# Key and value projections of a gated attention/MLP mix as units of seven block products, spilled and reloaded

## The chip, the cores and the metric

The kernel runs on one core of one Trainium2 chip. The metric is device time in microseconds (us) of one execution, given as the median of several runs; less is better. A profile shows one profiled execution: its span is the time from its first to its last instruction, and names such as L237 are lines of the kernel before.

## What is computed

The reference, cut to what matters (2048 tokens x 1024 channels, 32 heads of 32 channels, 3584 MLP channels, all in float32):

```python
x = A_x
g = _sigmoid((x * gate_w).sum(-1, keepdims=True))
q, k, v = split_heads(x @ wqkv)
pq, pk = q @ w_phi, k @ w_phi                      # per head
phi_q = concat([softmax(pq), softmax(-pq)])        # per head, 64 features
phi_k = concat([softmax(pk), softmax(-pk)])
kv = einsum("bhsf,bhsd->bhfd", phi_k, v)           # sum over all tokens
z  = einsum("bhsf->bhf", phi_k)
a = (phi_q @ kv / (phi_q @ z + 1e-6)) @ wo
b = (gelu(x @ w_gate) * (x @ w_up)) @ w_down
return g * a + (1 - g) * b
```

The features of every query need kv and z, which are sums over all 2048 tokens.

## The kernel before, in words

**Numbers.** Each float32 operand is split into a high part (rounded, written by ScalarE: `high`, L573, or `split`, L47) and a low part (the rest, written by VectorE: `low`, L576, or L48). A matrix product runs in three passes (`PASSES`, L24): high x high, high x low, low x high. One matmul has a stationary 128x128 block and 512 moving columns.

**Three stages.** The first stage (L165 to L560) projects keys and values. For each half of the heads (`hh`, L367) the weights for keys are folded with the feature map w_phi by small float32 matmuls (`fold`, L220) and stay split in SBUF; then sixteen chunks of 128 tokens are projected with the tokens on the output partitions (`keys_values`, L234: 8 blocks of channels x 3 passes x 2 column parts of 512). As the outputs are born in PSUM with tokens on partitions, `features` (L243) takes max, min, exponentials and normalisation right there, sums the features into `zacc` for z, and `accumulate` (L269) multiplies them with the values into four PSUM banks. The second stage projects queries, gate and up. The third multiplies by wo and w_down (L1189 on) and adds the gated results.

**Units of seven products.** In stages two and three a product of 2 x 2 blocks is made with seven block products instead of eight, from sums of blocks of x, of weights and of results (`x_sums` L174, `quarter_sums` and `more_sums` L156 to L163). A unit (`unit`, L947) is one pair of 128-channel column tiles of one weight (gate "g", up "u", query "q") for one half of the tokens (1024): seven calls of `product` (L908), each with 12 matmuls, so 84. Its weight operands are called x, y, z (1024 columns, split) and v (512). There are 64 units: half 0, then half 1, each 14 gate, 14 up and 4 query units. Operands of x for a half are four plain quarters (`xb`) and four sums (`xs`); at the turn `second_half` (L747) loads and splits those of half 1.

**What sets the order.** In stages two and three the order on TensorE (PE), VectorE (DVE), ScalarE (ACT) and SyncE (SP, which issues loads) is written out by a planner at build time. Time is counted in slots of one product, seven slots a unit. `run_slot` (L671) puts work of generator streams into each slot by estimated costs: `weights` (L789) prepares the operands of a unit from seven slots ahead to four slots behind its start, with due slots; `results` (L916) takes the products out; `background` (L1002) does work without a due slot when it fits, above all `attention` (L1042), a job for each of 8 head groups x 2 token blocks x 2 halves, 32 in all. Small matmuls of attention are "fillers" put into slots. What is left after the last unit runs in `drain` (L863), with no products beside it. In the second pass (half 1) the weight sums of the first pass are read back unsplit from HBM (`right_sums`) and split again. Spills to HBM go through GpSimd (POOL). The attention jobs read their queries back with `load_query` (L1033).

## Time and profile before

| | |
|---|---|
| median of 3 runs | 2352.43 us (2352.29 to 2352.74) |
| span of the profiled execution | 2351.2 us, 28278 instructions |
| HBM traffic | read 337.51 MB, written 109.58 MB, 190 GB/s |
| DMA packets | 156426, of these 22208 under 512 bytes |

The results give no separate device time for the profiled execution; its span lies 1.2 us under the median. On the page, an engine's line gives busy time, share of the span and number of instructions; a line of digits gives the busy tenths in 40 equal slices; PEclk is the clock granted to TensorE. A group's line reads: line, engine, operation, output tile <- input tiles, shapes, count, then total busy us and mean ns of one, then the idle time of the engine ahead of them and what ended it. In a row of windows the columns are the stretch, its length, then busy us (and instructions) of PE, PE weight loads, DVE, ACT and POOL, the granted clock, the DMA engines' busy share and GB/s.

### The profile page before, as it was taken

What the parts mean: (1) busy time and instruction counts of PE and PEld (TensorE: products, weight loads), DVE (VectorE), ACT (ScalarE), POOL (GpSimd) and SP (SyncE); (2) the same over time, 40 slices, a digit from 0 to 9 for tenths busy, and PEclk for the clock granted to TensorE, in tenths of its full rate; (3) what the DMA queues carried; (4) which work ended last, traced back from release to release, by engine and by line L of the source; (5) the groups of instructions that cost most, each with busy time, mean ns of one, the idle gap of its engine ahead of it and who ended that gap; (6) DMA issues with size and microseconds to landing.
All of it is one profiled execution on the core that took longest, in us unless ns stands there. A gap on an engine that the chain in (4) does not pass through costs nothing.

```text
span 2351.2 us, 28278 instructions
## 1 busy us (share of the span) xinstructions
PE 2346.5 (100%) x10594; PEld 1952.7 (83%) x10594; DVE 1808.1 (77%) x2356; ACT 1049.8 (45%) x1377; POOL 179.6 (8%) x334
## 2 busy tenths in 40 slices
PE   9999999999999999999999999999999999999999
PEld 8888888888888888888888888888888888888887
DVE  7997898887887777678778787787664868867874
ACT  4323223655555554456565655655533222323221
POOL 0000020211111111110001000000000000000000
PEclk9999999999999999999999999999999999999999
DMA  7322652645444655574444444444874767977874
GB/s 280 125 81 81 208 203 105 229 145 189 157 176 149 210 193 204 184 258 140 140 149 153 135 144 148 135 144 140 285 263 153 277 225 254 347 260 273 285 268 136
DMA packets 156426, 448.71 MB, mean 191 GB/s; under 512 B 22208, under 2 KB 24512, under 8 KB 155264
## 3 DMA queue, kind: packets, MB, share of 16 engines
q1 hardware_dynamic: 125664, 346.40, 44.2%
q0 software_dynamic: 29952, 100.17, 10.7%
q8 instruction: 83, 1.36, 0.2%
q10 hardware_dynamic: 672, 0.33, 0.1%
q14 instruction: 55, 0.45, 0.1%
HBM read 337.51 MB, written 109.58 MB: 190 GB/s over the span
## 4 chain that ended last, share of the span: by engine, by line
PE 100%; DVE 0%; issue 0%
PE po L1359 29%; PE a L913 22%; PE pd L237 15%; PE c L913 15%; PE b L913 7%; PE p L913 7%; PE pg L273 1%; PE misc L1132 1%; PE pd L609 0%; PE pd L150 0%; PE pg L225 0%; PE pd L225 0%; PE pd L197 0%; DVE x L1312 0%; DVE ones L187 0%
## 5 line engine op out<-in xcount | busy, mean ns | idle before, releaser
L237 PE MATMUL pd<-wkv,x 128*128 128x512 f32 x1536 | 358.6, 391 | 0.0
L237 PEld LDWEIGHTS pd<-wkv,x 128*128 128x128 f32 x1536 | 286.0, 188 | 57.4
L1359 PE MATMUL po<-tw,wgu 128*128 128x512 f32 x1344 | 309.8, 389 | 0.0
L1359 PEld LDWEIGHTS po<-tw,wgu 128*128 128x128 f32 x1344 | 252.3, 188 | 52.4
L573 ACT ACTIVATE wgu<-stage 128x1024 fp32r<-128x1024 f32 x146 | 154.2, 1056 | 245.3 <-DVE stage L1249 161.9
L576 DVE TENSOR_TENSOR wgu<-stage,wgu 128x1024 fp32r<-128x1024 f32 x146 | 177.8, 1218 | 83.0 <-ACT wgu L573 82.0
L576 DVE TENSOR_TENSOR tyz<-stage,tyz 128x1024 fp32r<-128x1024 f32 x129 | 156.9, 1216 | 67.9 <-ACT tyz L573 67.6
L913 PE MATMUL a<-s,tyz 128*128 128x512 f32 x768 | 184.6, 389 | 0.0
L913 PE MATMUL a<-s,v 128*128 128x512 f32 x768 | 184.5, 389 | 0.0
L913 PE MATMUL c<-x,tyz 128*128 128x512 f32 x768 | 184.5, 389 | 0.0
L913 PE MATMUL a<-x,wgu 128*128 128x512 f32 x756 | 181.7, 389 | 0.0
L913 PE MATMUL p<-s,tyz 128*128 128x512 f32 x756 | 181.6, 389 | 0.0
L913 PE MATMUL c<-x,wgu 128*128 128x512 f32 x756 | 181.6, 389 | 0.0
L913 PE MATMUL b<-s,tyz 128*128 128x512 f32 x756 | 181.6, 389 | 0.0
L913 PEld LDWEIGHTS a<-s,tyz 128*128 128x128 f32 x768 | 144.1, 188 | 30.1 <-ACT c L958 0.2
L913 PEld LDWEIGHTS a<-s,v 128*128 128x128 f32 x768 | 144.2, 188 | 29.9
L913 PEld LDWEIGHTS c<-x,tyz 128*128 128x128 f32 x768 | 144.2, 188 | 29.9
L913 PEld LDWEIGHTS p<-s,tyz 128*128 128x128 f32 x756 | 141.9, 188 | 29.5
L913 PEld LDWEIGHTS b<-s,tyz 128*128 128x128 f32 x756 | 141.9, 188 | 29.4
L913 PEld LDWEIGHTS c<-x,wgu 128*128 128x128 f32 x756 | 141.9, 188 | 29.5
L913 PEld LDWEIGHTS a<-x,wgu 128*128 128x128 f32 x756 | 141.8, 188 | 29.4
L1359 PE MATMUL po<-tw,wl 128*128 128x512 f32 x672 | 156.9, 389 | 0.0
(195 smaller groups left out, 3455.4 us busy)
## 6 DMA issues: line engine op xcount, KB each, us to landing
stage<-lm SPq DMA_DIRECT2D x98, 512.0 KB, 4.5
sr<-in_w_down SPq DMA_DIRECT2D x84, 512.0 KB, 5.1
sl<-lm SPq DMA_DIRECT2D x70, 512.0 KB, 4.7
lm<-h POOLq DMA_DIRECT2D x112, 256.0 KB, 2.3
stage<-in_w_gate SPq DMA_DIRECT2D x43, 512.0 KB, 3.7
stage<-in_w_up SPq DMA_DIRECT2D x43, 512.0 KB, 3.6
tg<-stage POOLq DMA_DIRECT2D x28, 512.0 KB, 2.9
tu<-stage POOLq DMA_DIRECT2D x28, 512.0 KB, 3.4
```

The costliest lines, as they stand in the source:

```text
L237: nc.tensor.matmul(ps[m], xb[b, kc // 4][:, a, kc % 4, t * P:(t + 1) * P], w[:, e, m * 512:(m + 1) * 512], start=kc == 0 and (a, e) == (0, ...
L273: nc.tensor.matmul(pkv[d // 2][:, d % 2], vs[:, d].rearrange("p a b -> p (a b)"), f[:, :, :, heads], start=first and d % 2 == 0, stop=last ...
L573: nc.scalar.activation(dst, src, AF.Copy)
L576: nc.vector.tensor_tensor(dst, src, dst_h.bitcast(F32), OP.subtract)
L913: nc.tensor.matmul(dst, w[:, h, 4 * part + kc, :], xq[:, e, kc, :], start=first and kc == 0 and i == 0, stop=kc == 3 and i == 2, skip_grou ...
L1132: nc.tensor.matmul(po[p], kbs[:, p].rearrange("p i a b -> p (i a b)"), pts[:, q, p, :], start=q == 0, stop=q == 1)
L1359: nc.tensor.matmul(ps[c], lefts[s][:, a, m, c * P:(c + 1) * P], made[k][:, e, m], start=d == 0 and m == 0 and n == 0, stop=d == n_duo - 1 ...
```

## The change

Keys ("k") and values ("v") become units like gate, up and query: four pairs of column tiles x two halves each. Their results are spilled to HBM with channels on partitions and brought back with tokens on partitions, by DMAs in pieces of 32 numbers plus 32x32 block transposes on VectorE. The list of units is now: half 0 v and k, half 1 v and k, half 1 gate/up/query, half 0 gate/up/query, so the operands of x change halves twice (`change_half`, the old `second_half`, is called at both turns). Unit 0 is a plain product (8 blocks of channels, no sums) run while x arrives and is summed. Behind it stand the folds of the key weights (`fold_piece`), in part within unit 1, and the first splits. The query folds, the gate's dot products, the sums of half 1 and the features of keys (`features`, now 32 jobs) are streams under the units; z is summed by accumulating DMAs into HBM and reduced in `finish_z`; `attention` waits for all of that. In `attention` the first steps of a job move to a stream of their own (`front`), and the four exponentials are placed one by one. The first pass of each weight pair stores y, z and v split; a second pass reads them back ready, and splits only x. The diff is cut to its core; what was in the first stage is left out.

```diff
+        for s in range(KC):
+            kc, i = kcs[s], s // 2
+            w_high, w_low = weight_part(s, 1 if s < 2 else 2) if s < 2 or s % 2 == 0 else (lambda: None, lambda: None)
+            xq = {blk: x_plain(blk, kc) for blk in range(2)}
+            src = {blk: raws[i][2 - 2 * blk + s % 2] for blk in range(2)}
+            w_high()
+            high(xq[1][:, 0], src[1])
+            if s == 0:
+                nc.vector.tensor_copy(xq[0][:, 0], src[0])
+            else:
+                high(xq[0][:, 0], src[0])
+            for blk in (1, 0):
+                low(xq[blk][:, 1], src[blk], xq[blk][:, 0])
+            w_low()
+            if s >= 2:
+                sum_steps(1)
+            if s % 2:
+                ready.append(i)
+            if s == 3:
+                for h in range(2):
+                    t = fp.tile([P, 4, 4, 32], F32, tag=f"vs{h}", name="bp", bufs=1)
+                    nc.vector.tensor_tensor(t, phi_c[:, 4 * h:4 * h + 4].unsqueeze(2).to_broadcast([P, 4, 4, 32]),
+                                            mask.unsqueeze(1).to_broadcast([P, 4, 4, 32]), OP.mult)
+                    bps.append(t)
+            for n, (a, e) in enumerate(PASSES):
+                for blk in (1, 0):
+                    for f in range(2):
+                        nc.tensor.matmul(plain_banks[blk, f], wide_w[a][:, kc, f * P:(f + 1) * P], xq[blk][:, e],
+                                         start=s == 0 and n == 0, stop=s == KC - 1 and n == 2)
...
+        def fold_piece(i):
+            h, kc = order[i]
+            s, pf = homes[i], misc()
+            for j in range(4):
+                nc.tensor.matmul(pf[:, j * P:(j + 1) * P], s[:, j * P:(j + 1) * P],
+                                 bps[h][:, j].rearrange("p a b -> p (a b)"), start=True, stop=True)
+            high(s, pf)
+            nc.gpsimd.dma_start(wk_fold[h][kc], s)
+            if 5 <= i < 12:
+                fold_load(i + 4)
...
+        sum_steps(100)
+        fold_piece(0)
+        plain_out(0, 1, 0)
+        fold_piece(1)
+        plain_out(1, 0, 1)
+        high(flat(x1)[0], first_e)
+        low(flat(x1)[1], first_e, flat(x1)[0])
+        fold_piece(2)
+        plain_out(2, 0, 0)
+        quarter_sums(first_e, first_o)
+        high(flat(y1)[0], first_o)
+        fold_piece(3)
+        plain_out(3, 1, 1)
+        low(flat(y1)[1], first_o, flat(y1)[0])
+        nc.gpsimd.dma_start(sums["v", 1]["y"], y1.rearrange("p a b c -> p (a b c)").bitcast(F32))
...
+        def plain_out(n, j, f):
+            high(results_0[:, n], plain_banks[j, f])
+            nc.gpsimd.dma_start(spilled["v"][0][f][j], results_0[:, n])
...
+        def more(n, m):
+            for _ in range(n):
+                x_highs.pop(0)()
+            for _ in range(m):
+                x_lows.pop(0)()
...
+        more(2, 0)
+        fold_piece(4)
+        more(2, 4)
+        fold_piece(5)
+        more(3, 3)
+        more_sums(first_e, first_o)
+        z1 = slot()
+        high(flat(z1)[0], first_e)
+        fold_piece(6)
+        low(flat(z1)[1], first_e, flat(z1)[0])
+        nc.gpsimd.dma_start(sums["v", 1]["z"], z1.rearrange("p a b c -> p (a b c)").bitcast(F32))
+        more(9, 9)
 
...
+        for half in (0, 1):
+            units += [(half, k, m) for k in "vk" for m in range(N_Q)]
+        for half in (1, 0):
             mine = [(half, k, m) for m in range(NF // 2) for k in "gu"]
             for m in range(N_Q):
-                mine.insert((0, 7, 12, 19)[m] if half else 7 * m, (half, "q", m))
+                mine.insert((0, 7, 12, 19)[m], (half, "q", m))
             units += mine
-
-        right_ops = {}
+        TURNS = [n for n in range(1, len(units)) if units[n][0] != units[n - 1][0]]
...
+            def load_parts(i, t):
+                nc.sync.dma_start(t.rearrange("p a b c -> p (a b c)").bitcast(F32), sums[kind, m][i])
             if n == 1:
-                ke, e, ko, o = 0, second_raw[0], 1, second_raw[1]
+                mine.update(x=x1, y=y1, z=z1)
             else:
-                while not room(2):
+                yield t - 7, t - 6, 0.0
+                while not room(1 + fresh):
                     yield now[0] + 1, t - 5, 0.0
-                ke, e = hold((0, 1024, w[2 * m]))
-                ko, o = hold((0, 1024, w[2 * m + 1] if fresh else right_sums[kind, m][0]))
-            yield t - 5, t - 3, 0.0, 1.05
-            x = new_weight() if n > 1 else xa.tile([P, 2, KC, P], F32R, tag="pts", name="second", bufs=1)
-            xh, xl = flat(x)
-            high(xh, e)
-            yield now[0] + 1, t - 2, 1.25
-            low(xl, e, xh)
-            mine["x"] = x
-            held[ke] = fresh
-            yield max(now[0], t - 4), t - 2, 1.4 if fresh else 0.0, 1.05
+                ke, e = hold(block(kind, 2 * m))
+                if fresh:
+                    ko, o = hold(block(kind, 2 * m + 1))
+                yield t - 5, t - 3, 0.0, 1.05
+                w = new_weight()
+                xh, xl = flat(w)
+                high(xh, e)
+                yield now[0] + 1, t - 2, 1.25
+                low(xl, e, xh)
+                mine["x"] = w
+                held[ke] = fresh
+                if fresh:
+                    yield max(now[0], t - 4), t - 2, 1.4, 1.05
+                    quarter_sums(e, o)
+                    y = slot()
+                    yh, yl = flat(y)
+                    high(yh, o)
+                    yield now[0], t - 1, 1.4
+                    more_sums(e, o)
+                    yield now[0] + 1, t, 1.25
+                    low(yl, o, yh)
+                    mine["y"] = y
+                    keep_parts("y", y)
+                    held[ko] = False
+                else:
+                    yield max(now[0], t - 4), t - 4, 0.0
+                    y = mine["y"] = slot()
+                    load_parts("y", y)
...
+            else:
+                yield t, t, 0.0
+                z = mine["z"] = slot()
+                load_parts("z", z)
...
+            else:
+                yield t + 5, t + 5, 0.0
+                v = mine["v"] = xa.tile([P, 2, KC // 2, P], F32R, tag="v", name="v", bufs=1)
+                load_parts("v", v)
...
+            while fjobs or jobs or between:
+                near = between and now[0] > between[0][0] - (10 if fjobs else 15)
+                if between and now[0] >= between[0][0]:
                     _, what, args = between.pop(0)
                     yield from what(*args)
-                    rest = now[0] + 6
-                elif jobs and now[0] >= jobs[0][0] and not (between and now[0] > between[0][0] - 10
-                                                            and between[0][1] is second_half):
+                elif fjobs and now[0] >= fjobs[0][0] and not near and not folding[0]:
+                    yield from features(fjobs, between)
+                elif not fjobs and finishing[0] == 1 and not near:
+                    yield from finish_z()
...
+        def load_tokens(dst, src):
+            v = src.rearrange("(j c) (t b r) -> b c t j r", c=32, b=4, r=32)
+            for b in range(4):
+                nc.sync.dma_start(dst[32 * b:32 * b + 32].rearrange("c (t j r) -> c t j r", t=4, j=4), v[b])
...
+                nc.vector.transpose(work[:, 1], shared["qx"])
...
+                nc.gpsimd.dma_start(z_sum[g], wide[1], **(dict(accum_op=OP.add) if half or j else {}))
...
+        def front(job, box):
+            load_query(*job)
+            yield now[0] + 2, NEVER, 0.0
+            few = lambda: room(2 if between else 1)
+            while not few() and not (idle[0] and lows[0]):
+                yield now[0] + 1, NEVER, 0.0
+            key, s = hold() if few() else (None, wide[1])
+            x, f = s[:, BLK:].rearrange("p (a b) -> p a b", b=32), s.rearrange("p (s a b) -> p s a b", s=2, b=32)
+            yield now[0], NEVER, 0.7
+            nc.vector.transpose(s[:, BLK:], shared["qx"])
+            yield now[0], NEVER, 1.4
+            mm = extremes
+            nc.vector.tensor_reduce(mm[:, 0, :], x, AX.X, OP.max)
+            nc.vector.tensor_reduce(mm[:, 1, :], x, AX.X, OP.min)
+            yield now[0], NEVER, 1.4
+            for i in range(2):
+                nc.vector.tensor_tensor(f[:, i], x, mm[:, i].unsqueeze(2).to_broadcast([P, 16, 32]), OP.subtract)
+            box.append((key, s))
...
+        extra = {k: [piece(i) for i in range(*r)] for k, r in ((0, (7, 9)), (1, (9, 10)), (2, (10, 13)), (4, (13, 16)))}
```

Here `sum_steps` issues the next sums of x on VectorE, and `x_highs` and `x_lows` are the sixteen high and low parts of 512 columns of the sums of x of half 0. `fold_piece` takes a bank with `misc()`, which alternates between two PSUM banks. Through `extra`, fold pieces 7 to 15 stand ahead of products of unit 1, the first of the units that `unit` issues. The planner (`run_slot`, `fits`), `product` and `results` are as before but for names; a filler may now stand in any slot of a unit but its first. The third stage begins with half 1 instead of half 0 and keeps its sums in other tiles.

1118 lines of the change are left out of this document (480 added, 638 removed).

## The prediction

> **What bounds the kernel now.** I read the page's busy times and slices first, then the chain that ended last, then the three stages by windows, then TensorE's instructions in order of time.
>
> ```profile
> PE 2346.5 (100%) x10594; PEld 1952.7 (83%) x10594; DVE 1808.1 (77%) x2356; ACT 1049.8 (45%) x1377; POOL 179.6 (8%) x334
> PE   9999999999999999999999999999999999999999
> PEclk9999999999999999999999999999999999999999
> PE 100%; DVE 0%; issue 0%
> PE po L1359 29%; PE a L913 22%; PE pd L237 15%; PE c L913 15%; PE b L913 7%; PE p L913 7%; PE pg L273 1%; PE misc L1132 1%; PE pd L609 0%; PE pd L150 0%; PE pg L225 0%; PE pd L225 0%; PE pd L197 0%; DVE x L1312 0%; DVE ones L187 0%
> ```
>
> TensorE (PE) is busy in every slice, its clock is full throughout, and the chain that ended last consists of matmuls. Busy alone can deceive, since the ends of matmuls are modelled, so I look at their spacing, inside a unit and at the start:
>
> ```profile
> 1642.88 2.88 PE L913 MATMUL c<-x,tyz 128*128 128x512 f32 x12
> 1645.60 2.88 PE L913 MATMUL a<-s,tyz 128*128 128x512 f32 x12
> 1.06 4.10 PE L197 MATMUL pd<-ones 128*128 128x128 f32 x18 [1.06 <-DVE ones L187]
> 4.92 3.81 PE L237 MATMUL pd<-wkv,x 128*128 128x512 f32 x12
> L237 PE MATMUL pd<-wkv,x 128*128 128x512 f32 x1536 | 358.6, 391 | 0.0
> ```
>
> One product of twelve matmuls starts 2.72 us after the one before: 2.72 / 12 = 0.2267 us for each 512-column matmul. The first real one starts at 4.92 us. So the time is the number of matmuls times their rate, plus two short ends; it changes by the matmuls removed and by pauses put between them. The stages, by windows (busy us of each engine):
>
> ```profile
> 0.00:414.30 414.30, 413.24 (x2067) 352.31 (x2068) 348.34 (x472) 138.05 (x178) 20.21 (x40) 1.00 0.46 156
> 414.30:1661.90 1247.60, 1247.60 (x5505) 1032.98 (x5504) 979.42 (x1402) 702.86 (x984) 143.15 (x264) 1.00 0.49 168
> 1661.90:2351.20 689.30, 685.62 (x3025) 567.38 (x3023) 480.31 (x482) 208.93 (x216) 16.21 (x30) 1.00 0.73 254
> ```
>
> Keys and values take the first, the 64 units of gate, up and query the second, the output products the third.
>
> **The matmuls: minus 40.8 us.** Keys and values now cost 1536 of the 512-column matmuls. After the change unit 0 is a plain product, 2 token blocks x 2 column tiles x 8 x 3 passes = 96. The other fifteen units have 7 products of 12, together 1260. That makes 1356, so 180 fewer, by 0.2267 us 40.8 us, all on the bounding engine. Accumulations stay 256, weight folds 256 records, attention 128, the last stage 3024; those that move from the first stage to slots between products ("fillers") cost the same there. The last stage changes only which half of the tokens comes first: I cost that at nothing, as its tiles are free before their first use.
>
> **The start: plus 0.5 us.** The first product now needs a 256 KB load of x where a 128 KB one did.
>
> ```profile
> early<-in_xT SPq DMA_DIRECT2D x2, 128.0 KB, 3.5
> 4.00:8.00 4.00, 4.00 (x16) 3.45 (x16) 3.27 (x10) 1.38 (x3) 0.00 (x0) 1.00 1.09 387
> ```
>
> At 387 GB/s another 128 KB is 0.3 us, and its high-part copy is 512 columns wide instead of 256. Bounds: 0 and 2 us; I take 0.5. After that each step of unit 0 needs 640 KB, 1.7 us at that rate, and lasts 12 x 0.2267 = 2.72 us, so loads keep ahead. Unit 0 ends at 4.92 + 0.5 + 21.8 = 27.2 us.
>
> **The block behind unit 0: plus 12.4 us.** This is where I expect part of the gain to go. Sixteen folds of key weights run there and in unit 1, on two PSUM banks in turn, so fold i waits until ScalarE (ACT) has copied out fold i-2. ACT is in program order, and its queue holds, mixed with the fold copies, four copies of unit 0's results, the high parts of x1, y1, z1, and sixteen high parts of sums of x.
>
> ```profile
> L225 PE MATMUL pg<-bd,early 128*128 128x128 f32 x64 | 8.3, 274 | 0.0
> 8.57 1.95 PE L225 MATMUL pg<-bd,early 128*128 128x128 f32 x16
> L47 ACT ACTIVATE wkv<-pg 128x512 fp32r<-128x512 f32 x8 | 4.8, 598 | 12.5 <-PE pg L225 12.5
> L573 ACT ACTIVATE tyz<-stage 128x1024 fp32r<-128x1024 f32 x129 | 136.1, 1055 | 37.5 <-DVE stage L158 28.4 <-PE c L913 7.4 <-PE a L913 1.3
> L576 DVE TENSOR_TENSOR tyz<-stage,tyz 128x1024 fp32r<-128x1024 f32 x129 | 156.9, 1216 | 67.9 <-ACT tyz L573 67.6
> L158 DVE TENSOR_TENSOR stage<-stage 128x512 f32<-128x512 f32 x34 | 23.5, 692 | 1.2
> ```
>
> A fold is 8 records, 8.3 x 8 / 64 = 1.04 us, say 1.05 with its start. Copies cost 0.60 (512 wide) and 1.055 (1024 wide). The queue moves from 27.2 + 1.05 = 28.3. Fold 6's copy has ahead of it 6 fold copies, 4 results and 7 sums, 17 x 0.60 = 10.2, and x1, y1, z1, 3.2. Two waits for VectorE (DVE) come in: y1 needs quarter_sums, which follow ten left-over sums (10 x 0.69 from about 22.5, as unit 0 has some 17.5 us for DVE: 16 low parts, 5 of weights, 6 sums, two masks) and x1's low part; that is ready 1.4 us after ACT asks. z1 needs more_sums, behind the low part of the seventh sum: 0.69 + 1.38 = 2.1 us. So fold 6 is out at 28.3 + 10.2 + 3.2 + 3.5 + 0.6 = 45.8. Fold 8 waits for it and stands ahead of unit 1's first product; TensorE, unhindered, would be there at 27.2 + 8 x 1.05 = 35.6. That is 10.2 us of pause, in pieces. Fold 9 then needs fold 7's copy, behind nine more sums: 45.8 + 5.4 + 0.6 = 51.8, where TensorE stands at 45.8 + 1.05 + 2.72 = 49.6: 2.2 more. Sum 12.4. Bounds: with neither DVE wait 8.9; with DVE 4 us later than I have it, 16.4. The folds' loads stand on the SP queue behind a load that waits for DVE's split of the seventh step, at about 20.5; 512 KB and nine times 256 KB at 387 GB/s are 7.4 us, each landing ahead of its fold.
>
> The trace has no pause of this length: PEclk stays at 9 in all slices. The Trainium skill ("TensorE: Matmul & The Clock Gate", HAM oscillation) says that a pause of TensorE over some 3.4 us puts it back to half clock. By that the longest pause here would cost up to 1.7 us more, an estimate from that page, and the sum would be 1.7 higher; no run here shows it yet.
>
> **DVE and ACT under the units.** They set the end only where they run out of room.
>
> ```profile
> L265 DVE TENSOR_TENSOR zacc<-zacc,e 128x1024 f32<-128x1024 f32 x30 | 36.7, 1225 | 1.0
> L48 DVE TENSOR_TENSOR x<-stage,x 128x1024 fp32r<-128x1024 f32 (+1 forms) x18 | 18.6, 1039 | 0.0
> L576 DVE TENSOR_TENSOR v<-stage,v 128x512 fp32r<-128x512 f32 x64 | 43.8, 684 | 1.5 <-ACT v L573 1.2
> L1054 DVE STREAM_TRANSPOSE x<-qx 128x512 f32<-128x512 f32 x32 | 22.6, 707 | 1.2 <-DMA xs<-x 0.8
> L927 DVE TENSOR_TENSOR h<-a,x 128x512 f32<-128x512 f32 x36 | 24.6, 685 | 18.5 <-PE a L913 18.5
> ```
>
> Removed: in the second pass the low parts of y, z and v come ready by DMA, 32 x (2 x 1.216 + 0.684) = 99.7; zacc 36.7 (now an accumulating DMA); splits of plain x 18.6. Added: seven fresh key/value units x (3 x 1.216 + 0.684 + 4 x 0.69 + 2 x 0.685) = 59.2; eight reloading ones x (1.216 + 1.37) = 20.7; one more change of half, 14 x 1.216 = 17; transposes of tokens, 64 x 0.707 = 45.2. Smaller ones left out, DVE has 348 + 979 - 155 + 142 = 1314 us in 1621: 81%, before 80%. ACT gains table loads only (about 30 x 1.3) and loses the second pass's high parts (32 x 2.7): no bound. POOL, 180 us busy now, gains some 230 issues (117 stores of split sums, 64 of keys and values, folds, accumulations); even at a microsecond each it is idle four fifths of the time. Covered, so nothing; without cover, the rivals.
>
> **DMA.** Key and value tiles come back as 256 loads of 64 KB in pieces of 128 bytes. The nearest rows are the loads of phi_c, also 64 KB in 128-byte pieces:
>
> ```profile
> phi_c<-in_w_phi ACTq DMA_DIRECT2D x1, 64.0 KB, 3.8
> phi_c<-in_w_phi SPq DMA_DIRECT2D x1, 64.0 KB, 6.3
> lm<-h POOLq DMA_DIRECT2D x112, 256.0 KB, 2.3
> stage<-tg SPq DMA_DIRECT2D x26, 512.0 KB, 3.4
> x<-xp SPq DMA_DIRECT2D x4, 2048.0 KB, 9.0
> ```
>
> ```profile
> 13.53 0.37 SPq L399 DMA_DIRECT2D phi_c<-in_w_phi  x1
> ```
>
> They landed in 3.8 and 6.3 us in the busiest part of the run, no slower than larger pieces. Eight of them per job, issued together and about a job ahead, cost nothing; one after the other, 30 to 50 us a job. Their issue on SP is 256 x 0.37 = 95 us over the whole run. The Trainium skill ("DMA: Bandwidth & Descriptors", Specifications) puts line rate at 512 bytes and up, and these are a quarter of that. The two rows show no collapse; the rule would feed the first rival below and is in its chance.
>
> **The sum.** 2351.2 - 40.8 + 0.5 + 12.4 = 2323.3 us of span. The median of the runs, 2352.43, lies 1.2 above the span of the profiled one, so 2324.5. Its own range, with the bounds above and a few us of small pauses, is 2318 to 2332.
>
> **Rivals.** *Attention is left over* (slower). Attention may start only when all 32 feature jobs are done, since it needs the sums over all tokens; what isn't done at the last unit runs in drain() with TensorE idle. How full is DVE there?
>
> ```profile
> 1440.00:1500.00 60.00, 60.00 (x266) 49.69 (x265) 46.68 (x69) 36.30 (x51) 3.78 (x7) 1.00 0.41 137
> 1440.00:1500.00 60.00, 1.42 (x2) 1.00 0.41 137
> 60.00:100.00 40.00, 40.00 (x189) 33.56 (x188) 37.87 (x48) 13.26 (x14) 0.00 (x0) 1.00 0.40 141
> L1067 ACT ACTIVATE x<-x 64x512 f32<-64x512 f32 x128 | 80.7, 631 | 22.2 <-DVE x L1062 20.6
> L1067 ACT ACT_TABLE_LOAD x30 | 38.5, 1283 | 0.5
> ```
>
> Now 60 us of the second pass hold two jobs (qx, second line) and 3.06 units, each unit 1.216 + 1.37 + 1.2 (up's products) for x and results and 3.1 for y, z, v, 6.9: a job takes (46.68 - 21.1) / 2 = 12.8 us of DVE. If attention starts only with the last 32 units, it needs 410 there, units and change of half 139: 549 of 638 us, 86%; two units later, 91%. For: now a job takes 30 us of wall time, and 32 must fit at about 19. Against: DVE ran 37.87 of 40 us without a pause of TensorE, and the job's front is split off to overlap. A job left over costs 12.8 (DVE alone) to 12.8 + 4 x 0.631 + 1.283 = 16.6 us. Against the 27.9 gained it decides from the third on; four give 2376 to 2391. Chance 0.13.
>
> *Late second-pass loads* (slower). z now comes as a 1 MB load issued at its unit's start and is used three products, 8.2 us, later; the SP queue's other loads wait ahead of it. Between 3.4 (512 KB) and 9.0 (2 MB), 1 MB lands by bytes in 5.3: hidden. At 9.0 each of 40 units would lose 0.8, together 34: 2358. Chance 0.06.
>
> *The start costs nothing* (ACT's copies slip ahead as TensorE needs them): 2351.2 - 40.8 + 1.2 = 2311.6, to 2317. The program order speaks against it. Chance 0.15.
>
> *Small pauses in the middle*, one job left over or some loads late: 2332 to 2347. Chance 0.11.
>
> **How the numbers follow.** The forecast has 0.55. About 0.2% (4.7 us) is what a measurement can tell here. Forecast, clean start and small pauses are all faster by more: 0.81, of which I give 0.02 back to same. Of the two slower rivals' 0.19, a quarter would land near the old time. The range 2311 to 2347 holds all but those two.
>
> **What would show it.** Right: 10594 - 180 = 10414 matmul records, with 96 of unit 0 and fifteen more units in place of the 1536; TensorE pauses between about 30 and 52 us at the fold line, released by ACT, 10 to 14 us together; then products every 2.72 us to the end; the last stage still 685 us. Wrong: idle TensorE just ahead of the last stage (attention left over), short pauses at each z product released by DMA, or a trace full from 5 us on (no loss at the start).

## The result and the profile after

The changed kernel takes 2489.07 us (median of 4 runs, 2479.82 to 2494.62) where the kernel before takes 2352.48 (2352.29 to 2352.74): 1.0576 times as long, 95% interval 1.0553 to 1.0598. Forecast were 2324.5 us, 2311 to 2347. The profiled execution took 2494.62 us, its span is 2492.8. From the page of the changed kernel: busy time, slices, packets and the chain that ended last.

```profile
PE 2361.8 (95%) x10414; PEld 1939.9 (78%) x10414; DVE 1823.8 (73%) x2460; ACT 1124.1 (45%) x1545; POOL 300.6 (12%) x526
PE   8778998999988889899999999999999999999999
PEclk8989999999999999999999999999999999999999
DMA  9999987788887778778656655555587576887784
DMA packets 340530, 626.80 MB, mean 251 GB/s; under 512 B 163216, under 2 KB 192160, under 8 KB 320416
HBM read 417.20 MB, written 207.89 MB: 251 GB/s over the span
PE 53%; DVE 16%; DMA 13%; issue 7%; ACT 7%; SPq 2%; POOL 1%; DVEq 0%; POOLq 0%; ACTq 0%
```

The 10414 matmul records are there: 180 fewer, as forecast. But TensorE has holes in the first seventeen slices, its clock dips, and the chain, once all PE, is PE for 53% only; 36% of it runs through DVE, DMA and ACT. The kernel before moved 448.71 MB, wrote 109.58 of them and had 22208 packets under 512 bytes. The same by windows (TensorE's busy us second; clock, DMA share and GB/s at the end):

```profile
0.00:240.00 240.00, 194.02 (x901) 163.12 (x902) 126.03 (x202) 89.90 (x146) 60.01 (x115) 0.90 0.94 336
240.00:1080.00 840.00, 776.98 (x3420) 634.89 (x3419) 635.87 (x868) 398.54 (x592) 160.82 (x264) 0.97 0.82 250
1080.00:1800.00 720.00, 702.23 (x3061) 572.16 (x3059) 580.20 (x909) 425.21 (x591) 63.62 (x118) 1.00 0.64 221
1803.50:2492.80 689.30, 685.58 (x3025) 567.36 (x3023) 480.41 (x482) 208.92 (x217) 16.19 (x30) 1.00 0.73 255
```

Width less busy is idle time: 46.0, 63.0 and 17.8 us in the first three stretches; the last stage is as it was, and only begins 142 us later (1803.5 for 1661.9). Over the whole span 2492.8 - 2361.8 = 131.0 us are idle, before 4.7. It is also busy 56 us longer than the matmuls call for (2361.8 against 2346.5 - 40.8 = 2305.7), and the clock makes most of that: at a mean of 0.981, 2361.8 x 0.019 = 45 us, an estimate. Idle time and slower matmuls, 126 and 56 us over before, are the 182 us by which the span missed 2351.2 - 40.8. Who TensorE waits for, and who ScalarE waits for, from the view of waits (us, times, longest):

```profile
ACT wgu L56 <- DMA stage<-in_w_gate: 97.8, 24, 8.7
ACT wgu L56 <- DMA stage<-in_w_up: 72.7, 19, 8.9
PE misc L727 <- DMA fold<-in_wqT: 31.4, 5, 9.8
PE misc L854 <- DVE pts L59: 24.9, 9, 4.7
PE b L616 <- ACT b L662: 24.0, 11, 5.9
PE misc L1053 <- DVE pts L59: 9.6, 14, 0.8
PE misc L1053 <- ACT pts L56: 6.9, 10, 0.8
```

TensorE names DVE and ACT, yet ACT's own longest waits are for weights: in the written order of ACT, the copy b<-a (L662) stands behind the split of a weight that has not landed. The start, where the prediction put its one loss, in order of time:

```profile
8.77 0.55 PE L257 MATMUL c<-x,wgu 128*128 128x512 f32 x1 [3.61 <-ACT x L56]
...
32.27 1.95 PE L277 MATMUL misc<-bp,stage 128*128 128x128 f32 x16
...
40.62 5.79 PE L277 MATMUL misc<-bp,w 128*128 128x128 f32 x24 [2.52 <-ACT fold L56]
49.55 1.66 PE L277 MATMUL misc<-bp,fold 128*128 128x128 f32 x8 [3.14 <-ACT w L56]
50.87 4.21 PE L616 MATMUL a<-x,wgu 128*128 128x512 f32 x12
```

Unit 0 ends at 32.3, not 27.2. From there to the end of the product behind the last folds, unit 1's fifth (71.84 + 2.72 = 74.56), are 42.3 us; sixteen folds and five products need 16 x 1.05 + 5 x 2.72 = 30.4. The block costs 11.9, forecast 12.4, and at the forecast place. But only 8.3 us of it are pauses (7.1 ended by ACT, 1.2 by a fold's load); the rest is TensorE at half clock, as in the 5.79 us for the 24 matmuls of three folds, which take 3 x 1.05 at the full rate.

### The profile page after: what moved, and what is told of

Its sections match the earlier page's. It is cut to its first block, busy times and chain, and to the rows that moved or that the text cites. A ratio compares the mean times of both kernels' runs of the same rounds, so it can differ in the third digit from the quotient of the medians.

```text
span 2492.8 us, 29222 instructions
## 1 busy us (share of the span) xinstructions
PE 2361.8 (95%) x10414; PEld 1939.9 (78%) x10414; DVE 1823.8 (73%) x2460; ACT 1124.1 (45%) x1545; POOL 300.6 (12%) x526
## 2 busy tenths in 40 slices
DMA packets 340530, 626.80 MB, mean 251 GB/s; under 512 B 163216, under 2 KB 192160, under 8 KB 320416
## 3 DMA queue, kind: packets, MB, share of 16 engines
HBM read 417.20 MB, written 207.89 MB: 251 GB/s over the span
## 4 chain that ended last, share of the span: by engine, by line
PE 53%; DVE 16%; DMA 13%; issue 7%; ACT 7%; SPq 2%; POOL 1%; DVEq 0%; POOLq 0%; ACTq 0%
PE po L1300 27%; PE a L616 10%; PE c L616 7%; DMA stage<-in_w_gate 4%; PE b L616 4%; DMA stage<-in_w_up 3%; PE p L616 3%; SPq L784 2%; ACT L991 1%; ACT w L991 1%; DMA fold<-in_wqT 1%; DVE wgu L59 1%; DVE h L598 1%; DVE pts L59 1%; ACT pts L56 1%
## 5 line engine op out<-in xcount | busy, mean ns | idle before, releaser
L56 ACT ACTIVATE wgu<-stage 128x1024 fp32r<-128x1024 f32 (+2 forms) x168 | 175.2, 1043 | 500.8 <-DVE stage L1190 160.5
L59 DVE TENSOR_TENSOR wgu<-stage,wgu 128x1024 fp32r<-128x1024 f32 (+2 forms) x168 | 201.5, 1200 | 152.3 <-ACT wgu L56 149.3
L616 PE MATMUL b<-s,tyz 128*128 128x512 f32 x936 | 232.0, 398 | 24.1 <-ACT b L662 24.0
L616 PE MATMUL a<-s,tyz 128*128 128x512 f32 x948 | 237.4, 401 | 14.7 <-DMA tyz<-tk3z 4.3
L616 PE MATMUL a<-x,wgu 128*128 128x512 f32 x948 | 238.3, 402 | 0.0
L616 PE MATMUL a<-s,v 128*128 128x512 f32 x948 | 229.5, 391 | 0.0
L616 PE MATMUL c<-x,wgu 128*128 128x512 f32 x948 | 229.1, 391 | 0.0
L1300 PE MATMUL po<-tyz,wgu 128*128 128x512 f32 x672 | 155.2, 389 | 0.0
L1300 PEld LDWEIGHTS po<-tyz,wgu 128*128 128x128 f32 x672 | 126.1, 188 | 26.2
L1300 PEld LDWEIGHTS po<-tw,wl 128*128 128x128 f32 x672 | 126.1, 188 | 26.2
```

The lines of the kernel that those rows point to most:

```text
L56: nc.scalar.activation(dst, src, AF.Copy)
L59: nc.vector.tensor_tensor(dst, src, dst_h.bitcast(F32), OP.subtract)
L616: nc.tensor.matmul(dst, w[:, h, 4 * part + kc, :], xq[:, e, kc, :], start=first and kc == 0 and i == 0, stop=kc == 3 and i == 2, skip_grou ...
L1300: nc.tensor.matmul(ps[c], lefts[s][:, a, m, c * P:(c + 1) * P], made[k][:, e, m], start=d == 0 and m == 0 and n == 0, stop=d == n_duo - 1 ...
```

## The experiments

The theory after this reading: loads that come late hold up engines that work in a written order, and a late load has two causes, more bytes (some 100 MB of split sums y, z and v stored in the first pass and read back) and a longer queue ahead of it on SyncE (SP), where each token tile is now four DMAs of 512 pieces. Rivals: the bytes alone; the accumulating stores; half clock alone.

**Four leave-outs, each on the changed kernel.**

```diff
e1_no_split_stores   (and every reload reads sums["v", 1])
-                if again:
+                if again and n == 1:
e2_whole_tokens      (load_tokens: one load of 2 KB rows)
-            for b in range(4):
-                nc.sync.dma_start(dst[32 * b:32 * b + 32].rearrange("c (t j r) -> c t j r", t=4, j=4), v[b])
+            nc.sync.dma_start(dst, src)
e3_z_plain
-                nc.gpsimd.dma_start(z_sum[g], wide[1], **(dict(accum_op=OP.add) if half or j else {}))
+                nc.gpsimd.dma_start(z_sum[g], wide[1])
e4_fewer_rows        (13 of the gate's 16 loads of x rows left out)
-                    for i, r in enumerate(rows[:S // P - c]):
+                    for i, r in enumerate(rows if c == 0 else []):
```

> The split operands y, z, v are not stored to HBM after unit 1's (97 MB of writes go); all second uses read unit 1's copy, so the later products are of the wrong weights. Volume theory (TensorE waits because the DMA engines are full of bytes and loads land later than the planner allows): 2390 to 2420 us, the DMA share of the first 1080 us falls from 0.85-0.95 to about 0.7 and weight loads land in about 5 us instead of 6.8. Piece theory (the 128-byte token loads clog the SP queue): no more than 20 us gained, 2465 to 2490, since no token load changes.

> Each key or value tile comes back by one load of 256 KB in 2 KB rows instead of four of 64 KB in 128-byte pieces, so the tokens stand in the wrong places in the features. Piece theory: the loss after 300 us goes for the most part, 2390 to 2420. Volume theory: the same bytes, 2465 to 2490.

> The 32 accumulating stores of features for z become plain stores, so z holds the last block alone. If accumulating is what fills the engines or delays VectorE: 2440 or less. Volume theory: the 17 MB of read-back are gone, some 10 us at most, 2470 to 2490.

> 13 of the 16 loads of rows of x for the gate are left out (6.8 MB of the 98 MB of the first 300 us), so most gates are wrong. Volume theory: 6.8 MB at 335 GB/s are 20 us, nearly all of it seen, 2463 to 2475, and the gain lies ahead of 240 us. Piece theory, and the theory that the order on TensorE and ScalarE at the start is the main loss: no change, 2480 to 2495.

Measured: 2428.07 us (2427.01 to 2429.13) without the split stores, 2431.60 (2427.44 to 2435.76) with whole token loads, 2469.77 (2468.51 to 2471.04) without accumulation, 2484.75 (2482.45 to 2487.05) with fewer rows. So 61, 57, 19 and 4 us come back, and no one cause is enough. e1 writes 99.6 MB less. e1 and e2 gave 8 and 12 us less than the least their theories said. The 6.8 MB of rows left out were 20 us of transfer at the rate of the early stretch and gave 4, which is within the spread of the changed kernel's own runs: bytes have no fixed price. Why accumulating costs 19 us was not followed up; its stores land in 7.6 us (median) and plain ones in 6.4.

**The pair, the queue, and the converse.** e5 keeps four loads per tile but with rows of 2 KB; e6 keeps the pieces but issues them on GpSimd's queue; e7 is e1 and e2 together; b1 is the kernel *before* with the same kind of split sums stored for nobody.

```diff
e5_four_whole
-                nc.sync.dma_start(dst[32 * b:32 * b + 32].rearrange("c (t j r) -> c t j r", t=4, j=4), v[b])
+                nc.sync.dma_start(dst[32 * b:32 * b + 32], src[32 * b:32 * b + 32])
e6_pool_tokens
-                nc.sync.dma_start(dst[32 * b:32 * b + 32].rearrange("c (t j r) -> c t j r", t=4, j=4), v[b])
+                nc.gpsimd.dma_start(dst[32 * b:32 * b + 32].rearrange("c (t j r) -> c t j r", t=4, j=4), v[b])
b1_more_stores       (kernel before, weights(); z and v likewise)
             mine["y"] = y
+            if half == 0:
+                nc.gpsimd.dma_start(extras[kind, m]["y"], y.rearrange("p a b c -> p (a b c)").bitcast(F32))
```

> The changed kernel with the keys and values brought back in four loads of 64 KB each, as in the change, but with rows of 2048 B in place of pieces of 128 B (128 descriptors for 512 KB of issue work in place of 512 per load; the tokens stand in the wrong places, so the features that come out are those of other elements). Theory A (what costs is SyncE's time to issue 512 pieces per load, with the weight loads queued behind): the gain of the single whole load, 57 us, comes nearly all back if the issue of a load of few rows is short: 2425 to 2445. Theory B (what costs is the number of load instructions and their waits): little comes back, 2475 to 2490.

> The changed kernel with the same token loads, the same bytes and the same pieces of 128 B, issued from GpSimd's queue in place of SyncE's. Theory A (the weight loads wait behind the token loads in SyncE's order): most of the 57 us comes back, 2430 to 2450, unless GpSimd's stores then stand behind the token loads. Rival B (the small pieces slow all transfers in the engines, whoever issues them): nothing comes back, 2475 to 2500.

> The changed kernel without the split stores and with whole token loads, the two edits that gave 61 and 57 us alone (later products take a wrong weight, tokens stand in wrong places). If they are two separate costs they add up: 2489 - 118 = 2371, range 2360 to 2380. If they are one cost (both take up the same slack of the loads, and either edit is nearly enough) the pair gives little more than one: 2410 to 2428. If what is lost grows with the load faster than in proportion, the second edit gives less than the first: 2380 to 2405.

> The kernel before, with the split right-hand sums of 31 units of the first pass also stored, 1 MB, 1 MB and 0.5 MB each on GpSimd's queue into tensors that nobody reads: 81 MB more written, nothing else changed. Theory A (the stores alone crowd out the weight loads): the first pass loses in proportion to the 61 us that leaving out 97 MB gave in the changed kernel, 51 us: 2390 to 2420. Rival B (they cost only beside the change's other transfers): within 10 us of 2352.

Measured: e5 2467.76 (2467.25 to 2468.28), e6 2424.83 (2422.41 to 2427.25), e7 2393.80 (2392.24 to 2395.37), b1 2354.31 (ratio 1.0006, interval 0.9995 to 1.0017). The pair (e7) gives 95 us, less than the 118 of both alone: they share slack. e5 missed both expectations and lies between them. What SP spends on one token DMA explains it, from the views of the loading line of the changed kernel, e5 and e2 (min/median/max ns):

```profile
L784 SPq DMA_DIRECT2D w<-vt x128: 557/636/2739, 274.6 to 940.8; - x128
```
```profile
L783 SPq DMA_DIRECT2D w<-vt x128: 302/420/2531, 273.6 to 920.2; - x128
```
```profile
L782 SPq DMA_DIRECT2D w<-vt x32: 319/320/327, 272.2 to 875.4; - x32
```

The medians hide long ones. Summed over all token DMAs of the trace, SP spends 217.3, 138.2 and 21.5 us on them, for 2489, 2468 and 2432 us in all: 79.1 us less of SP gives 21, 195.8 less gives 57, that is 0.27 and 0.29 us for each microsecond of SP. Between e5 and e2 only the number of DMAs differs, and that alone is 36 us. A rival is that SP stands at the token DMAs because the tile they fill is not free yet, with the weight loads behind: the view of waits has 354.8 us of this in the changed kernel. But it has 446.4 us in e2, where the 57 us come back all the same. e6 keeps all bytes and takes the loads out of SP's order; 64 us come back, 0.30 for each of the 217.3, and the middle stretch closes though more flows per second:

```profile
0.00:240.00 240.00, 191.51 (x888) 160.89 (x889) 123.58 (x200) 87.17 (x142) 62.18 (x118) 0.89 0.93 332
240.00:1080.00 840.00, 830.35 (x3756) 687.57 (x3755) 689.66 (x934) 442.74 (x651) 357.89 (x536) 1.00 0.86 280
```

Idle from 240 to 1080 us falls from 63.0 to 9.7, at 280 GB/s instead of 250. Here not the bytes were short, but SP's time in front of other loads. Weight loads hardly land sooner in e6, from issue to landing; they go out sooner, and ACT's waits for gate and up weights fall from 170.5 to 92.7 us. Landing times in the median, of before, the changed kernel and e6:

```profile
stage<-in_w_gate SPq DMA_DIRECT2D x43, 512.0 KB, 3.7
stage<-in_w_gate SPq DMA_DIRECT2D x42, 512.0 KB, 6.8
stage<-in_w_gate SPq DMA_DIRECT2D x42, 512.0 KB, 6.4
```

How one such load does it, in the changed kernel in order of time:

```profile
732.34 2.96 SPq L784 DMA_DIRECT2D w<-vt  x4
...
735.39 1.79 SPq L64 DMA_DIRECT2D stage<-in_w_gate  x2
...
742.28 1.06 ACT L56 ACTIVATE wgu<-stage 128x1024 fp32r<-128x1024 f32 x1 [5.23 <-DMA stage<-in_w_gate]
...
746.71 0.59 ACT L662 ACTIVATE b<-a 128x512 f32<-128x512 f32 x1
...
747.35 3.02 PE L616 MATMUL b<-s,tyz 128*128 128x512 f32 x12 [2.27 <-ACT b L662]
```

SP is 3 us at four token DMAs, the weight load goes out behind them and lands 6.9 us after its issue began, ACT waits 5.2 us at its split, the copy behind that split is late, and TensorE stands 2.3 us. b1 shows the other side, 480 to 1080 us of the kernel before with 81 MB more to write:

```profile
480.00:1080.00 600.00, 599.40 (x2643) 495.74 (x2643) 461.80 (x641) 318.82 (x446) 127.25 (x238) 1.00 0.82 310
```

310 GB/s, and 0.6 us idle: bytes alone cost the kernel before nothing at a DMA share of 0.82.

**Asking earlier, and where bytes do count.** What is left in e6 is the first 240 us, where DMA is at 0.93. e8 asks for the query folds earlier; e9 was to put attention products later; e10 is e6 with e1; e11 is e6, e8 and e9 together.

```diff
e8_fold_lead
                 nc.sync.dma_start(s, wqT[g][:, cols])
-                yield now[0] + 2, NEVER, 0.0
+                yield now[0] + 6, NEVER, 0.0
...
                 folding[0] -= 1
-                yield now[0] + 1, NEVER, 0.0
+                yield now[0] + 3, NEVER, 0.0
e9_attend_later
-                    fillers.append((passed[0], attend, 4, range(1, 7)))
+                    fillers.append((passed[0] + 2.0, attend, 4, range(1, 7)))
```

> The changed kernel with one thing other: a query fold's weights are asked for six slots ahead of its products in place of two, and the next load into the same tile comes three slots behind the store in place of one. Theory (the early loss is TensorE standing in its written order at loads that were asked for too late): the 31 us of waits at the query folds go, and with them the half clock behind them, 10 to 15 us: 2440 to 2450. Rival (the engines of the DMA are full at 0.93 to 0.97 up to 240 us, so another wait takes the place): 2475 to 2490.

> The changed kernel with one thing other: an attention job's four products are put into TensorE's order 2 us later by the planner's own account than it holds them to be ready. The trace shows waits of 16.5 us in 24 at these products, none over 1 us, while 27 us are lost between 1080 and 1800 us. Theory A (a pause of under 1 us costs more than itself, since the clock falls to half for some us behind it): more comes back than the waits, 20 to 27 us: 2462 to 2470. Theory B (a pause costs itself alone): 14 to 17 us, 2472 to 2476. If the later products leave attention over for the end, the time does not fall: 2485 or more.

> The changed kernel with the token loads on GpSimd's queue and without the split stores (later products take a wrong weight). The first edit alone gave 2425. Theory A (bytes: 97 MB less written are worth 61 us whatever else is in the queues): 2360 to 2370. Theory B (81 MB more cost the kernel before nothing, so the stores cost only while SyncE's order is held up; with the token loads out of it they cost little): 2412 to 2425. As the pair without split stores and with whole tokens went, 38 us: 2387.

> The changed kernel, all that it computes kept, with three things of order other: token loads on GpSimd's queue, query folds' loads six slots ahead, attention products 2 us later. Theory (bytes cost nothing here, only late loads and the half clock behind each pause do): from 2425 the 33 us at the query folds, the 15 us at the attention products and 35 to 45 us of half clock behind these go; what is left is the block behind the first unit, some 19 us, and little else: 2330 to 2345, under the kernel before. Rival (the bytes are what is short, and the waits move to other loads): 2380 to 2425.

Measured: e8 2513.74 (2511.97 to 2515.50), e9 2494.20 (2492.30 to 2496.11), e10 2391.01 (2389.49 to 2392.53), e11 2454.74 (2451.19 to 2458.29). e9 tells nothing but how a repeat comes out: its edit left the order of every engine as it was. e10 gives 34 us over e6, neither the 61 that the stores were worth alone nor next to nothing. The theory behind e8 and e11 fell; both lie above their rivals' ranges too. In e8 (waits, then order of time at the end) the query folds no longer wait, but something else does:

```profile
PE b L616 <- ACT b L662: 55.3, 16, 9.2
PE misc L1053 <- ACT pts L56: 33.0, 11, 16.1
```
```profile
1806.92 0.80 PE L1053 MATMUL misc<-pts,kbs 128*128 128x512 f32 x1 [16.14 <-ACT pts L56]
...
1820.65 0.79 PE L1053 MATMUL misc<-pts,kbs 128*128 128x512 f32 x1 [10.82 <-ACT pts L56]
```

The waits at the copy behind the weights' splits grew from 24.0 to 55.3 us, and ACT's own waits for up weights from 72.7 to 106.0: the earlier fold loads took their turn from others. And since features begin when the folds are done, everything behind came later, and two attention jobs were left for the end, 16.1 and 10.8 us. That is the prediction's first rival, near its price of 12.8 to 16.6 us a job, made by this experiment and not by the change.

**Only the early part, and the converse with both.** e12 leaves the split stores out in units 2 to 10 only, up to about 240 us. Of these only units 2 to 7 store any: 15.7 MB less is written (207.89 to 192.16), a sixth of the 99.6 and not the 23.6 MB, a quarter, of the two expectations. e13 does so with e6's queue and e4's rows. b2 and b3 add to before and to b1 two copies per unit, in the first 32 units, each as four DMAs in pieces of 128 bytes on SP, between tensors in memory.

```diff
e12_early_stores_out (and later reloads of these read sums["v", 1])
-                if again:
+                if again and (n == 1 or n > 10):
b2_token_issues      (called ahead of each of two steps of last_weight, n < 32)
+        def copy_pieces():
+            src = xT[0:P, 0:1024].rearrange("p (a r) -> p a r", r=64)
+            dst = dram.tile([P, 16, 64], F32, name=f"cp{next(copies)}")
+            for b in range(4):
+                nc.sync.dma_start(dst[32 * b:32 * b + 32, :, :32], src[32 * b:32 * b + 32, :, :32])
```

> The changed kernel with the split stores left out of units 2 to 10 alone, the first 240 us, 23.6 MB of the 97 MB (their later products take a wrong weight). The stretches up to 240 us lost 66 us, 49 when all split stores were out. Theory A (bytes cost only where the DMA engines are full, at 0.93 and more, that is up to 240 us): the gain is 16 to 25 us, and nothing changes behind: 2463 to 2473. Theory B (bytes cost everywhere alike): a quarter of 61 us, 2474 and the loss of every later stretch as it was. If the whole 61 us came from here: 2428.

> The changed kernel with token loads on GpSimd's queue (2425), the split stores left out of units 2 to 10, and 13 of the 16 loads of x rows for the gate left out (wrong weights and wrong gates). All split stores out gave 2391 there. Theory A (with SyncE's order free of the token loads, bytes cost only up to 240 us): the early part of the stores is worth as much as all of them, 25 to 34 us, and the rows some 5 us: 2385 to 2397. Theory B (bytes cost alike everywhere): a quarter of 34 us and 4 us: 2410 to 2415.

> The kernel before, with two copies added per unit to each of its first 32 units, each as four DMAs of 64 KB in pieces of 128 B on SyncE's queue, between tensors in memory that nothing else uses: 256 DMAs as the changed kernel's token loads, issued with no wait. Theory A (the issue time of such a load, 0.6 us each, holds up the weight loads behind it): weight loads come up to 2.6 us later, which costs the kernel before something too: 2360 to 2400. Rival (the kernel before has enough lead to bear one such load at a time; its weight loads land in 3.7 us where the changed kernel's take 6.8): 2352 to 2358.

> The kernel before with both additions: 81 MB of split sums stored for nobody on GpSimd's queue (alone 2354), and the 256 DMAs in pieces of 128 B on SyncE's queue. Theory (a late weight load is the sum of a slower landing and a longer queue, and costs only when the two pass the lead of about 5 us): more than both alone, 2370 to 2420. Rival (the costs are separate): what the second edit gives alone plus 2 us.

Measured: e12 2471.42 (2468.84 to 2473.99), e13 2397.43 (2394.16 to 2400.69), b2 2358.00 (2354.34 to 2359.07), b3 2384.68 (2383.69 to 2385.67). e12 first, beside e1's middle stretch:

```profile
0.00:240.00 240.00, 208.46 (x982) 174.91 (x983) 141.80 (x219) 102.92 (x161) 53.33 (x102) 0.94 0.88 296
240.00:1080.00 840.00, 779.51 (x3425) 637.79 (x3424) 634.83 (x870) 400.57 (x595) 161.88 (x264) 0.97 0.81 250
```
```profile
240.00:1080.00 840.00, 810.89 (x3636) 669.55 (x3636) 668.67 (x912) 425.32 (x628) 116.23 (x180) 0.99 0.62 170
```

A sixth of the stores gives 18 us where its share of the 61 would be 10, and it is gained ahead of 240 us, where idle time falls from 46.0 to 31.5; behind, it stays at 60.5. With all stores out (e1) it fell to 29.1 there: while SP is held up, bytes count in the middle too. With SP free they hardly do (9.7 us in e6, 6.4 in e10). In e13 this sixth of the stores and the rows, 22.5 MB, were worth 27 us, where all stores, 99.6 MB, were worth 34 in e10: most of what bytes still cost, they cost early. First stretch of e13, then of e10:

```profile
0.00:240.00 240.00, 217.58 (x1024) 183.30 (x1025) 145.78 (x224) 108.27 (x169) 57.13 (x108) 0.94 0.83 282
```
```profile
0.00:240.00 240.00, 209.26 (x997) 175.67 (x998) 143.81 (x221) 104.94 (x164) 56.05 (x106) 0.95 0.88 301
```

Idle there falls from 48.5 (e6) to 22.4 and 30.7. b1 alone cost 1.4 us, b2 alone 5.3 (3.2 of it idle time between 240 and 480 us), both together 32: the costs are not separate. 480 to 1080 us of before, of b2 and of b3:

```profile
480.00:1080.00 600.00, 600.00 (x2648) 496.78 (x2647) 462.99 (x644) 319.26 (x446) 82.64 (x153) 1.00 0.53 187
```
```profile
480.00:1080.00 600.00, 600.00 (x2648) 496.70 (x2647) 463.25 (x641) 317.79 (x444) 83.38 (x154) 1.00 0.69 210
```
```profile
480.00:1080.00 600.00, 582.06 (x2530) 478.33 (x2529) 445.34 (x621) 298.61 (x419) 127.22 (x237) 0.98 0.98 329
```

The kernel before has 0.53 of the DMA engines busy there at 187 GB/s, b1 0.82, b2 0.69, b3 0.98. In this stretch next to nothing is lost up to 0.82, and 17.9 us at 0.98. So b2 also says that SP's time on token DMAs is no cost by itself: SP spends 176.8 us on its copies, and before has lead enough to bear it, with weight loads landing in 3.9 us (median), while the changed kernel's take 6.8. What makes the lead too short in the changed kernel is, as far as these runs go, the sum of slower landing and longer queue: e1 shortens the landing (5.1), e2 and e6 the queue. That sum was not measured by itself, and b3 does not settle it: the changed kernel has a share of 0.80 in this stretch, not 0.98, and in b3 the issue slows too (0.846 us for a copy in the median, 0.627 in b2).

**The short waits at attention products.** e14 puts these products one product later in e6's order; e15 does so in e13.

```diff
                 def push(attend=attend):
-                    yield now[0], NEVER, 0.0
+                    yield now[0] + 1, NEVER, 0.0
                     fillers.append((passed[0], attend, 4, range(1, 7)))
```

> The changed kernel, all that it computes kept, with token loads on GpSimd's queue (2425) and an attention job's four products one product later in TensorE's order (the 2 us of an earlier trial had left the order as it was). There 14.4 us in 21 waits of at most 0.8 us stand at these products. Theory A (a pause under 1 us costs more than itself, since half clock follows): 20 to 30 us come back, 2395 to 2405. Theory B (it costs itself alone): 12 to 15 us, 2410 to 2413. If attention is then left over for the end, as with the folds asked for earlier: 2425 or more.

> The same with the split stores of units 2 to 10 and 13 of 16 rows for the gate also left out (2397 without the later products; wrong weights and gates). If the three causes (early bytes, SyncE's order, attention products that come too early) are all there is beside the start, what is left is the predicted 2324 and some 20 to 45 us of the first 240 us: 2345 to 2375. If there is another cause: 2385 or more.

Measured: 2408.56 (2406.38 to 2410.74; ratio to before 1.0238, interval 1.0208 to 1.0268), and 2380.06 (2379.66 to 2380.46). Both waits at L1053 are gone. 1080 to 1800 us of e6, then of e14:

```profile
1080.00:1800.00 720.00, 705.26 (x3055) 574.60 (x3054) 577.94 (x891) 416.35 (x576) 54.71 (x101) 0.99 0.63 217
```
```profile
1080.00:1800.00 720.00, 714.32 (x3133) 586.53 (x3132) 589.88 (x904) 420.03 (x583) 55.54 (x103) 1.00 0.65 226
```

78 more matmuls fit in, 78 x 0.2267 = 17.7 us: 9.1 us less idle, some 5 us of half clock less (e6 has three such stretches of 3.4 us here, each behind a pair of these waits, e14 none), and matmuls that start late. A gain of 16 for 14.4 us of waits lies between the two theories, and with runs that spread by 4 to 5 us it does not decide between them. Nor is it the products' alone: the edit shifts the planner's order elsewhere too, and ACT's waits for gate and up weights fall from 92.7 to 23.2 us. e14 is the fastest version that computes all the reference asks for; it is still 56 us slower than before. No version tried beats the kernel before. e15 is 5 us above its expectation: some 56 us over the forecast stay with all three causes eased. Its span has 45.9 us of idle time, 28 more than the forecast held (4.7 + 0.5 + 12.4), and TensorE is busy 26.5 us longer than the matmuls call for, of which a clock of 0.994 makes some 14.

## Why the prediction was wrong, step by step

- **Matmuls, minus 40.8: right.** 10414 records, and a last stage of 689.30 us as before.
- **Start, plus 0.5: wrong by size.** The first product began at 8.77, not 5.4. ACT issues six loads of its own first, the last at 6.09 us, and only then loads a table, which the step had left out:

```profile
6.09 0.37 ACTq L191 DMA_DIRECT2D phi_c<-in_w_phi  x1
6.49 1.28 ACT L56 ACT_TABLE_LOAD   x1 [6.49 <-DMA stage<-in_wv]
```

  Unit 0 then ran from 8.77 to 32.27, 23.5 us instead of 21.8: behind the 3.61 us pause its first matmuls came every 0.43 us instead of 0.23, up to 12.1. Together 5.1 us late.
- **Block behind unit 0, plus 12.4: right in the sum, in part by luck.** 11.9 measured, and ACT's copies are what TensorE waits for. But the forecast was pauses alone, 10 to 14 us of them; measured are 8.3, and half clock, which the sum left out, makes up the rest.
- **DVE and ACT under the units, nothing: right in the sum, not in the wait.** DVE is busy 73%, and attention was not left over. But 16.5 us of waits at attention products were not foreseen: TensorE's written order put them up to 0.8 us ahead of DVE and ACT. Nor were 24.9 us at the features' products (L854), released by DVE; they fall to 0.9 in e6, so they too hang on SP's order.
- **"DMA ... cost nothing": the step that failed.** It priced a token DMA by one load alone at the start of the run, 0.37 us on SP; in the middle it takes 0.636 in the median, and all 256 take 217 us instead of 95. More than the size, the question was wrong: not how long SP is busy in all, but which load stands behind those four, with what lead. A weight's load is issued two slots, 5.4 us, ahead of its split, and lands in 6.8 us where it took 3.7. Taking the loads off SP brought 64 us back.
- **Bytes: never summed.** The prediction listed stores for POOL's issue time alone and did not set their 100 MB against the stretches they fall in. At 336 GB/s and a share of 0.94 up to 240 us they cost: with SP free, e13 puts 22.5 MB of early bytes at 27 us, where e10 puts all stores at 34. Later, at a share of 0.82, 81 MB cost before nothing (b1).
- **Half clock: mechanism right, size off.** Priced at 1.7 us for one pause, it took 45. The rule of the Trainium skill ("TensorE: Matmul & The Clock Gate", HAM oscillation) that a pause of some 3.4 us or more brings half clock agrees with these rows of the changed kernel:

```profile
160.95 2.98 PE L616 MATMUL b<-s,tyz 128*128 128x512 f32 x12
...
173.70 2.05 PE L727 MATMUL misc<-w,fold 128*128 128x128 f32 x8 [9.78 <-DMA fold<-in_wqT]
...
175.41 5.01 PE L616 MATMUL a<-x,wgu 128*128 128x512 f32 x12
...
180.26 1.09 PE L616 MATMUL p<-s,tyz 128*128 128x512 f32 x4
```

Behind a pause of 9.8 us a product takes 180.26 - 175.41 = 4.85 us (less the fold's end, all of it matmuls) instead of 2.72. Other rows do not keep to 3.4 us, and there the measurement decides. Behind a pause of 2.21 us a product of the changed kernel takes 371.90 - 367.48 = 4.42 us, at a clock of 0.50; in e6 one takes 1385.89 - 1381.86 = 4.03 us behind two pauses of 0.84 and 0.76 us close together; and a pause of 3.4 us at 846.8 us brings no half clock. The step was wrong to apply the rule to one pause, and to long pauses alone.
- **The 512-byte rule** (Trainium skill, "DMA: Bandwidth & Descriptors", Specifications) was given a share of a chance on the ground that two loads showed no collapse. b2, whose copies stay within memory, shows a price: 0.16 more of the DMA engines for 23 GB/s more, where before 0.53 carry 187, two and a half times as much per byte.
- **Rivals.** The one whose direction came true is late loads (0.06), but it stood on z's reloads, which cost TensorE 14.7 us in all (4.3 the longest), not on weights behind token loads. The forecast and every rival counted one mechanism at a time, and none put a price on the weight loads behind the token DMAs.

The split of the 165 us between forecast and result depends on the order in which causes are removed: SP's order 64, then attention products 16, then early bytes 29, the rest 56. The 19 us of accumulating stores lie somewhere among these. The rest is placed in part (21.5 us idle up to 240 us, 14.0 up to 1080) but not settled.

## What to carry to other kernels

Before costing a transfer at nothing, write down for each stage its bytes per microsecond against what the DMA engines carry, and for each queue what stands behind the new issue and with what lead; a share of busy time answers neither. A pause of a few microseconds, or two short ones close together, can cost its length and then half speed for some more. Where each of two additions is free, try both at once.

## What the runs showed that was not expected

The same 131072 pieces of 128 bytes are 131072 small packets on SP's queue, and none on GpSimd's. The packets of e6, beside 163216 under 512 bytes in the changed kernel:

```profile
DMA packets 213554, 626.80 MB, mean 259 GB/s; under 512 B 32144, under 2 KB 61088, under 8 KB 193440
```

163216 - 32144 = 131072. So e6 removed the small packets as well as SP's time. e5, which removes the small packets, keeps four issues on SP and shortens them, gave 21 of e6's 64 us. From e5 to e2 the small packets stay away and only SP's time goes, by 116.7 us: that gave 36, 0.31 for each microsecond, where e5 gave 0.27. So no price of the small packets beside SP's time shows here.
